# A lane inverse's last three copies and the next compaction are handed out later, at a raised pace

## The chip, the cores and the metric

One core of one Trainium2 chip runs the whole program as a single launch. The metric is the device time of that launch in microseconds (us), the median of three executions. The core has a matrix engine (TensorE, PE in the profile), three engines for elementwise work (VectorE or DVE, ScalarE or ACT, GpSimd or POOL), a queue that issues DMAs (SyncE, SP) and 16 DMA engines. Each engine works through its own queue in the order in which the program put instructions there.

## The reference, cut to what matters

Three parts follow one another. The first is a delta rule over 4 batches, 8 heads and 768 steps with 48-wide states:

```
for t in range(S):
    y[:, :, t] = einsum('bhd,bhde->bhe', q[:, :, t], state)
    v_old      = einsum('bhde,bhd->bhe', state, kt)
    state      = state + beta_t * einsum('bhd,bhe->bhde', kt, vt - v_old)
```

Its output, turned to 3072 tokens by 384, goes through an RMS norm and a gated feed-forward (`silu(xn @ w_gate) * (xn @ w_val) @ w_out`, inner width 1536), and then through a second feed-forward (`h = x @ w_in`, `h * tanh(softplus(h)) @ w_out`, inner width 2048). All of it is float32.

## The kernel before, in words

The 768 steps are cut into 12 rows of 64 steps (r = 0 to 11); two rows are a segment (sg = 0 to 5). Within a row the recurrence is solved with matrices. It needs, for each segment, the inverse of 32x32 triangular blocks for all heads. From segment 2 on that inverse is made by the lane generator `inlane(sg)`, nearly all of it on DVE: a compaction of the matrix A (`diagonal`, ACT at L621 and DVE at L622, into the tile comp), a transpose into N_, a scaling, small steps of 2 to 7 (below called s2 to s7), products and reduces of 8x8 blocks (p8 and r8, L653 and L689), products and reduces of 16x16 blocks (p16 and r16, L653 and L707), a scaling mulX (L709), a transpose into X11 (L714), a transpose into yc (L718), and last three ACT copies of yc into A (L720 to L722). Each step ends with a `yield` of a cost; one segment's yields add up to 31.45. Straight after the copies of one segment comes the compaction of the next. `merges(sg)` then makes, on PE with ACT copies between, the off-diagonal blocks (`merge32`: L734, an ACT copy Z at L738, L744, an ACT copy into A at L748); its four parts are handed out between the first steps of the next segment's inverse.

`chain_row(r)` is a row's own work, as a list of named stages. Those that matter here: r (residual, L935 on PE and L940 on DVE), q0 and q1 (transposes of the queries at L615, copied by ACT at L616), p (scores, L595 and DVE L605), nA and nB (norms of the keys of row r+4; nB ends with a DVE reciprocal at L555 and a POOL product at L556), c0 and c1 (transposes of those keys, L615), y (L953), X and Y (the former row's output to the feed-forward, L1054; ACT L1058 and L1060, POOL L1061 writes xl), v (L978, ACT L983), k (state update, L1027 on PE and L1032, tile sx, on DVE), o0 and o1 (L994), g (L595 and ACT L603).

`part_a` is the feed-forward of earlier rows for the first 512 inner columns: matmuls at L255 to L257 into two-step tiles pg and pv (DVE L313 and L316 and POOL L317 make hh and hl from them), and a down product at L289 to L291 in three units that share one PSUM tile pd; ACT copies pd into par (L1110) before the next unit may write pd.

For each row from 2 to 9 `merge` interleaves these streams: it always takes the stream whose handed-out cost is the smallest share of that stream's total. The row's chain has its own cost as total, `part_a` 11 units, and the lane `P["LANE"]`, 15.7 = 31.45 / 2. `until` stops the lane for a row once its running total has reached `upto`, which is 14.2 for row 2 and 15.7 more for each row after, and without limit in row 9. The order that results is the order of every engine's queue; nothing is reordered later. PSUM tiles of the chain come from five banks (tag pp): a matmul into a reused bank waits for whoever read it last.

After row 11 (at about 460 us) the kernel runs the rest of the gated feed-forward and the second feed-forward, with matmuls throughout.

Of the kernel before, what the change touches and what calls it, by code (L numbers as in the profile page):

```python
# [17 lines left out]


P = dict(  # L20
    XB=2, WE=16, RB=4, TB=3, LANE=15.7, CVT=9.0, CVB0=0, CVB1=1.238, CVC=4.4, PSD=1, NU=6, CVA=1, CVE=14.671, CVD=3.5, SQ=5,
    ROW="r nA q0 q1 S p T nB y X v Y k c0 o0 c1 o1 g".split(),
    R0="r q0 q1 p v k o0 o1 s0 s1 x0 x1 c0 c1 g".split(),
    R1="r nA q0 q1 y p nB v k o0 o1 s0 s1 x0 c0 c1 g".split(),
# [37 lines left out]
def merge(*streams):  # L62
    live = [[g, float(total), 0.0] for g, total in streams if total > 0]
    while live:
        s = min(live, key=lambda x: x[2] / x[1])
        try:
            s[2] += next(s[0])
        except StopIteration:
            live.remove(s)


def budget(gen, amount):
    done = 0.0
    while done < amount:
        try:
            w = next(gen)
        except StopIteration:
            return
        done += w
        yield w  # L80


def until(gen, total, target):
    while total[0] < target:
        try:
            w = next(gen)
        except StopIteration:
            return
        total[0] += w
        yield w  # L90


def delay(amount):
    for _ in range(int(amount)):
        yield 1.0
# [3 lines left out]
def kernel(  # L99
# [18 lines left out]
    NR = S // C  # L118
# [7 lines left out]
    QE = 3  # L126
    XB = P["XB"]

    def pool(name, bufs=1, **kw):
        kw.setdefault("reuse_waits", "tile")  # L130
        return tc.tile_pool(name=name, bufs=bufs, **kw)
# [11 lines left out]
    def seq(*gens):  # L143
        for g in gens:
            yield from g


    def prepare(get_pool, key, cut, act=True, low=None, **kw):
        return [prepare_half(half, get_pool, key, cut, act, low or nc.gpsimd, kw) for half in range(2)]
# [50 lines left out]
    def convs(pairs, at_once=0):  # L200
        depth = P["RB"]
        gens = [g for p in pairs for g in p]
        for g in gens[:depth]:
            next(g)
        yield 0.1
        for g in gens[:at_once]:
            next(g)
            yield 0.2
        for g in gens[:at_once]:
            next(g)  # L210
            next(g)
            yield 1.4
        for i, g in enumerate(gens[:at_once]):
            for g in gens[i + depth:i + depth + 1]:
                next(g)
            for _ in gens[i]:
                pass
            yield 0.1
        gens = gens[at_once:]
        next(gens[0])  # L220
        yield 0.2
        last = iter(())
        for i, g in enumerate(gens):
            if i + 1 < len(gens):
                next(gens[i + 1])
            for _ in range(2):
                next(g)
                yield 0.7
            if i + depth < len(gens):
                next(gens[i + depth])  # L230
            for _ in last:
                pass
            last = g
            yield 0.1
        for _ in last:
            pass

    def cols(w, m):
        return w.rearrange("(k p) f -> p k f", p=128)[:, :, m * 256:(m + 1) * 256], KD, 256

    def rows(w, m):
        return w.rearrange("(k p) f -> p k f", p=128)[:, 2 * m:2 * m + 2, :], 2, DM
# [4 lines left out]
    def need(*keys):  # L247
        assert done.issuperset(keys), set(keys) - done
# [80 lines left out]
    def x_tiles():  # L329
        return [xp.tile([128, KD, T], F32R, tag=tag, name=tag, bufs=XB) for tag in ("xh", "xl")]  # L330

# [6 lines left out]
    def phase_b1():  # L338
# [33 lines left out]
        even, odd, top = (qc[:, 192 + i:193 + i] for i in range(3))  # L372
        bnat = xp.tile([128, KD, T], F32R, tag="xl", name="bnat", bufs=XB).bitcast(F32)
        bnat = bnat.rearrange("p a b -> p (a b)")[0:32, 0:S]
# [40 lines left out]
        def flat(t):  # L415
            return t.bitcast(F32).rearrange("p a b -> p (a b)")
# [209 lines left out]
        def inlane(sg):  # L626
# [89 lines left out]
            yc = il.tile([128, 1024], F32, tag="pr", name="yc", bufs=2)  # L716
            Yc = yc.rearrange("p (u c) -> p u c", c=32)
            nc.vector.transpose(out=Yc.rearrange("p u c -> p c u"), in_=Nv)  # L718
            yield 2.0
            nc.scalar.copy(A[32:64, :, 32:64], Yc[32:64])  # L720
            nc.scalar.activation(out=A[:, :, 0:32], in_=Yc, func=ACTF.Copy, scale=h0[:, 0:1])
            nc.scalar.copy(A[96:128, :, 32:64], Yc[96:128])  # L722
# [169 lines left out]
        def lanes(ending):  # L892

            nc.gpsimd.memset(X_, 0.0)
            nc.gpsimd.memset(X_.rearrange("p (i x) -> p i x", x=33)[:, :, 0:1], 1.0)
            for sg in range(2, NSEG):
                done_of, due = 0.0, 2.5
                for w in inlane(sg):
                    yield w
                    done_of += w  # L900
                    if done_of >= due:
                        next(ending, None)
                        due += 2.0
                for _ in ending:
                    pass
                ending = merges(sg)
            left.append(ending)

        def chain_row(r):
# [135 lines left out]
            def to_x(bp):  # L1045
                need(("sx", r, bp))
                po, dg = xn[bp]
                if bp == 0:
                    need(*([("up", r - XB)] if r >= XB else []))
                    x_t[r].extend(x_tiles())  # L1050
# [52 lines left out]
        def cost(r):  # L1103
            return sum(cost_of(x) for x in order(r))
# [42 lines left out]
        spare = rp.tile([128, 16, 64], F32, tag="PT", name="spare")[:, :, 0:D]  # L1147
        sq = [xp.tile([128, KD, T], F32R, tag="xh", name="sq", bufs=XB) for _ in range(2)]
        sq = [flat(t)[:, 0:16 * D].rearrange("p (u d) -> p u d", d=D) for t in sq]
# [26 lines left out]
        for sg in range(1, NSEG):  # L1176
            for rl in range(2):
                r = 2 * sg + rl
                streams = [(chain_row(r), cost(r))]
                due = P["DUE"][r] if r < len(P["DUE"]) else P["DUE"][-1]  # L1180
                if due > 0:
                    off = 1.5 if r == 2 else 0
                    streams.append((seq(delay(off), budget(part_a, due)), off + due))
                if r < len(P["CVS"]):
                    streams.append((budget(cv, P["CVS"][r]), P["CVS"][r]))
                if r < len(P["CVS"]):
                    streams.append((budget(cv, P["CVS"][r]), P["CVS"][r]))
                if sg + 1 < NSEG:
                    upto = (r - 1) * P["LANE"] - 1.5 if r < NR - 3 else 999.0
                    streams.append((until(lane, laned, upto), P["LANE"]))  # L1190
                elif rl == 0:
                    st_i.close()
                    streams.append((seq(left.pop(), delay(7.0)), 13.0))
                    wbp.append(st_b.enter_context(pool("wbA")))
                    todo = [(c, m, cols(w, m)) for m in range(FA, NP1) for c, w in (("g", w_gate), ("v", w_val))]
                    todo += [("o", m, rows(w_out1, m)) for m in range(FA, NP1)]
                    gens = []
                    for i, (c, m, cut) in enumerate(todo):
                        if 2 * i < WE:
                            gens.append(prepare(lambda: wbp[0], (c, m), cut, tag="wb", bufs=WE))  # L1200
                        else:
                            gens.append(prepare(lambda: wbp[1], (c, m), cut, low=nc.vector, tag="wb", bufs=2 * len(todo) - WE))
                    cv = convs(gens)
                    streams.append((budget(cv, 0.75 * WE), 0.75 * WE))
                else:
                    streams.append((budget(cv, 0.75 * WE), 0.75 * WE))
                merge(*streams)
# [136 lines left out]
    WE = P["WE"]  # L1344
    with tc.manual_schedule():
        st_b, st_w, st_2 = ExitStack(), ExitStack(), ExitStack()
        rest = [phase_b1()]
        w2i = st_2.enter_context(pool("w2i", side="right"))
        tpc = st_2.enter_context(pool("tpc", side="right"))
        ps_u = st_2.enter_context(pool("ps_u", P["NU"], space=PSUM))  # L1350
        ps_d = st_2.enter_context(pool("ps_d", 8 - P["NU"], space=PSUM))
        last = phase_c()
        phase_b2(rest[0], lambda: next(last))
        st_w.close()
        for _ in last:
            pass
        st_2.close()
        st_b.close()
# [30 lines left out]
```

## Time and profile before

| | us |
|---|---|
| median of three executions | 1211.27 (1210.17 to 1212.03) |
| the profiled execution | 1213.2, its span 1211.1 |
| PE busy in the span | 1125.3 (93%) |
| DVE busy | 713.1 (59%) |
| ACT busy | 566.7 (47%) |
| POOL busy | 400.4 (33%) |

The span is the time from the first to the last instruction of the profiled execution. Shares over the whole span mix a first part (to about 460 us), in which all engines take part, with a second in which PE is busy nearly always. The granted clock is the clock that TensorE was given, 1.00 for 2.4 GHz and 0.50 for 1.2 GHz.

### The profile page before, as it was taken

What the parts mean: (1) busy time and instruction counts of PE and PEld (TensorE: products, weight loads), DVE (VectorE), ACT (ScalarE), POOL (GpSimd) and SP (SyncE); (2) the same over time, 40 slices, a digit from 0 to 9 for tenths busy, and PEclk for the clock granted to TensorE, in tenths of its full rate; (3) what the DMA queues carried; (4) which work ended last, traced back from release to release, by engine and by line L of the source; (5) the groups of instructions that cost most, each with busy time, mean ns of one, the idle gap of its engine ahead of it and who ended that gap; (6) DMA issues with size and microseconds to landing.
All of it is one profiled execution on the core that took longest, in us unless ns stands there. A gap on an engine that the chain in (4) does not pass through costs nothing.

```text
span 1211.1 us, 33707 instructions
## 1 busy us (share of the span) xinstructions
PE 1125.3 (93%) x14784; PEld 1095.4 (90%) x14784; DVE 713.1 (59%) x1148; ACT 566.7 (47%) x1075; POOL 400.4 (33%) x360
## 2 busy tenths in 40 slices
PE   5687698999998879999999999999999999999998
PEld 5677687889897878999999999989999999999998
DVE  6657898798868767555555553379334433333433
ACT  4355636566555654211121111054757655555672
POOL 2031134354522443234443433223323322232232
PEclk7666788999999979999999999999999999999999
DMA  9022333232224544333333322331011101111101
GB/s 161 3 67 54 96 81 68 68 94 73 77 60 116 170 132 144 105 116 126 126 119 105 105 92 92 120 130 53 27 40 41 40 18 38 38 40 40 40 1 27
DMA packets 120483, 95.08 MB, mean 79 GB/s; under 512 B 79856, under 2 KB 102896, under 8 KB 120336
## 3 DMA queue, kind: packets, MB, share of 16 engines
q1 hardware_dynamic: 108240, 69.32, 21.2%
q10 hardware_dynamic: 12096, 23.60, 6.0%
q8 instruction: 116, 1.90, 0.7%
q14 instruction: 31, 0.25, 0.1%
HBM read 64.59 MB, written 28.31 MB: 77 GB/s over the span
## 4 chain that ended last, share of the span: by engine, by line
PE 70%; DVE 17%; ACT 5%; issue 4%; POOL 2%; DMA 1%; SPq 1%; DVEq 0%; POOLq 0%; ACTq 0%
PE pd L1285 5%; PE pd L1286 5%; PE pd L1284 5%; PE ph L256 5%; PE ph L257 5%; PE ph L255 5%; PE pd L289 4%; PE pg L255 4%; PE pd L291 4%; PE pd L290 3%; PE pg L257 3%; PE pg L256 3%; PE pv L255 3%; PE pv L256 3%; PE pv L257 3%
## 5 line engine op out<-in xcount | busy, mean ns | idle before, releaser
L1332 POOL TENSOR_TENSOR gl<-t,gh 128x512 fp32r<-128x512 f32 x96 | 124.6, 1298 | 272.0 <-DVE gh L1331 269.9
L317 POOL TENSOR_TENSOR hl<-sg,hh 128x512 fp32r<-128x512 f32 x72 | 98.7, 1370 | 241.8 <-DVE hh L316 233.5
L255 PE MATMUL ph<-xh,wih 128*128 128x256 f32 x576 | 162.0, 281 | 2.9 <-DVE t L1328 2.9
L257 PE MATMUL ph<-xh,wil 128*128 128x256 f32 x576 | 162.0, 281 | 0.0
L256 PE MATMUL ph<-xl,wih 128*128 128x256 f32 x576 | 161.9, 281 | 0.0
L289 PE MATMUL pd<-hh,woh 128*128 128x256 f32 x420 | 122.3, 291 | 15.0 <-ACT par L1110 15.0
L1285 PE MATMUL pd<-wql,gh 128*128 128x384 f32 x384 | 129.6, 337 | 0.3
L1284 PE MATMUL pd<-wqh,gh 128*128 128x384 f32 x384 | 129.4, 337 | 0.5 <-DVE wqh L195 0.5
L1286 PE MATMUL pd<-wqh,gl 128*128 128x384 f32 x384 | 129.3, 337 | 0.0
L255 PE MATMUL pg<-xh,wgh 128*128 128x256 f32 x432 | 128.6, 298 | 0.3 <-ACT wgh L193 0.3
L307 ACT ACTIVATE sg<-pg 128x512 f32<-128x512 f32 x72 | 43.1, 598 | 183.1 <-PE pg L257 161.2
L255 PE MATMUL pv<-xh,wvh 128*128 128x256 f32 x432 | 126.4, 293 | 0.0
L257 PE MATMUL pg<-xh,wgl 128*128 128x256 f32 x432 | 124.8, 289 | 0.9 <-DVE wgl L196 0.9
L256 PE MATMUL pg<-xl,wgh 128*128 128x256 f32 x432 | 124.7, 289 | 0.8 <-POOL xl L1061 0.8
L257 PE MATMUL pv<-xh,wvl 128*128 128x256 f32 x432 | 122.4, 283 | 1.1 <-DVE wvl L196 1.1
L256 PE MATMUL pv<-xl,wvh 128*128 128x256 f32 x432 | 122.5, 284 | 0.0
L290 PE MATMUL pd<-hl,woh 128*128 128x256 f32 x420 | 119.7, 285 | 0.0
L291 PE MATMUL pd<-hh,wol 128*128 128x256 f32 x420 | 119.6, 285 | 0.0
L1328 DVE TENSOR_TENSOR t<-t,ph 128x512 f32<-128x512 f32 x96 | 65.2, 679 | 82.1 <-ACT t L1326 82.1
L255 PEld LDWEIGHTS ph<-xh,wih 128*128 128x128 f32 x576 | 109.2, 190 | 3.1 <-DVE t L1328 3.1
L313 DVE TENSOR_TENSOR sg<-sg,pv 128x512 f32<-128x512 f32 x72 | 49.4, 686 | 102.5 <-PE pv L257 96.4
L256 PEld LDWEIGHTS ph<-xl,wih 128*128 128x128 f32 x576 | 109.1, 189 | 0.0
(213 smaller groups left out, 2913.0 us busy)
## 6 DMA issues: line engine op xcount, KB each, us to landing
raw<-in_moe_w_out_dram SPq DMA_DIRECT2D x28, 384.0 KB, 3.5
raw<-in_moe_w_in_dram SPq DMA_DIRECT2D x16, 384.0 KB, 4.1
kh<-in_k_dram SPq DMA_DIRECT2D x24, 192.0 KB, 3.9
qp<-in_q_dram SPq DMA_DIRECT2D x24, 192.0 KB, 3.6
v<-in_v_dram SPq DMA_DIRECT2D x48, 96.0 KB, 3.1
raw<-in_moe_w_gate_dram SPq DMA_DIRECT2D x12, 384.0 KB, 3.3
raw<-in_moe_w_val_dram SPq DMA_DIRECT2D x12, 384.0 KB, 3.7
xh_d<-xh SPq DMA_DIRECT2D x12, 384.0 KB, 2.4
```

The lines of the kernel that those rows point to most:

```text
L255: nc.tensor.matmul(ps[:, f, :], wh[:, kt, sl], xh[:, kt, :], start=(kt == 0), stop=False)
L256: nc.tensor.matmul(ps[:, f, :], wh[:, kt, sl], xl[:, kt, :], start=False, stop=False)
L257: nc.tensor.matmul(ps[:, f, :], wl[:, kt, sl], xh[:, kt, :], start=False, stop=(kt == KD - 1))
L289: nc.tensor.matmul(ps, wh[:, f, sl], hh[:, f, :], start=(i + f == 0), stop=False)
L290: nc.tensor.matmul(ps, wh[:, f, sl], hl[:, f, :], start=False, stop=False)
L291: nc.tensor.matmul(ps, wl[:, f, sl], hh[:, f, :], start=False, stop=last)
L317: nc.gpsimd.tensor_tensor(out=hl, in0=sg, in1=hh.bitcast(F32), op=ALU.subtract)
L1284: nc.tensor.matmul(ps, gh[:, f, sl], wh[:, f, :], start=(m + f == 0), stop=False)
L1285: nc.tensor.matmul(ps, gh[:, f, sl], wl[:, f, :], start=False, stop=False)
L1286: nc.tensor.matmul(ps, gl[:, f, sl], wh[:, f, :], start=False, stop=last)
L1328: nc.vector.tensor_tensor(out=t, in0=t, in1=ps, op=ALU.mult)
L1332: nc.gpsimd.tensor_tensor(out=gl, in0=t, in1=gh.bitcast(F32), op=ALU.subtract)
```

## The change

The yield after the transpose into yc grows from 2.0 to 8.2, the pace LANE from 15.7 to 18.8 (half of the new sum 37.65), and the constant by which `upto` falls short of the pace from 1.5 to 3.0. So `upto` is 15.8 for row 2 and 18.8 more for each row after. No instruction is added or removed.

```diff
-    XB=2, WE=16, RB=4, TB=3, LANE=15.7, CVT=9.0, CVB0=0, CVB1=1.238, ...
+    XB=2, WE=16, RB=4, TB=3, LANE=18.8, AFTER=6.2, LD=3.0, CVT=9.0, CVB0=0, CVB1=1.238, ...
...
             nc.vector.transpose(out=Yc.rearrange("p u c -> p c u"), in_=Nv)
-            yield 2.0
+            yield 2.0 + P["AFTER"]
             nc.scalar.copy(A[32:64, :, 32:64], Yc[32:64])
...
                 if sg + 1 < NSEG:
-                    upto = (r - 1) * P["LANE"] - 1.5 if r < NR - 3 else 999.0
+                    upto = (r - 1) * P["LANE"] - P["LD"] if r < NR - 3 else 999.0
                     streams.append((until(lane, laned, upto), P["LANE"]))
```

## Rows read from the trace of the kernel before

**Rows 1.** Waits of PE, 160 to 450 us: waited for, us in total, times, longest.

```profile
PE pd L289 <- ACT par L1110: 13.2, 4, 4.3
```

**Rows 2.** PE in order of time: start, us, instruction, count, [idle before <- releaser].

```profile
200.46 1.04 PE L615 MATMUL pp<-ident,qp 128*128 128x128 f32 x8
205.53 0.58 PE L289 MATMUL pd<-hh,woh 128*128 128x256 f32 x1 [4.04 <-ACT par L1110]
...
269.17 0.39 PE L289 MATMUL pd<-hh,woh 128*128 128x256 f32 x1 [2.45 <-ACT par L1110]
...
328.49 0.39 PE L289 MATMUL pd<-hh,woh 128*128 128x256 f32 x1 [2.42 <-ACT par L1110]
...
383.18 1.20 PE L734 MATMUL pp<-X,A 32*32 32x32 f32 x64 [1.06 <-DVE X L714]
...
388.90 0.24 PE L744 MATMUL pp<-A,Z 32*32 32x32 f32 x2 [2.91 <-ACT Z L738]
```

**Rows 3.** ACT in order of time, at the start of row 4.

```profile
200.79 1.04 ACT L720 COPY A<-yc 32x1024 f32<-32x1024 f32 x1 [4.05 <-DVE yc L718]
...
204.07 1.15 ACT L621 ACTIVATE comp<-A,h 128x1024 f32<-128x1024 f32 x1
```

**Rows 4.** DVE in order of time: the first yc, and sx of rows 4, 6, 8.

```profile
198.69 2.07 DVE L718 STREAM_TRANSPOSE yc<-N__166 128x1024 f32<-128x1024 f32 x1
...
228.13 1.02 DVE L1032 TENSOR_TENSOR sx<-sx,pp 128x384 f32<-128x384 f32 x2 [7.74 <-PE pp L1027]
...
287.44 1.02 DVE L1032 TENSOR_TENSOR sx<-sx,pp 128x384 f32<-128x384 f32 x2 [4.11 <-PE pp L1027]
...
348.86 1.02 DVE L1032 TENSOR_TENSOR sx<-sx,pp 128x384 f32<-128x384 f32 x2 [8.91 <-PE pp L1027]
```

**Rows 5.** Stretches: length, busy PE, PEld, DVE, ACT, POOL, granted clock, DMA, GB/s.

```profile
165.00:200.00 35.00, 34.04 (x745) 31.45 (x744) 34.62 (x40) 18.96 (x51) 16.68 (x15) 0.99 0.33 76
...
205.00:210.00 5.00, 4.47 (x72) 4.24 (x74) 4.71 (x4) 2.86 (x7) 0.51 (x1) 0.50 0.02 4
210.00:215.00 5.00, 5.00 (x122) 4.68 (x120) 3.09 (x11) 1.53 (x3) 3.69 (x3) 0.63 0.01 3
...
330.00:335.00 5.00, 5.00 (x141) 4.62 (x140) 4.06 (x5) 1.77 (x4) 0.00 (x0) 0.68 0.02 3
...
460.00:1211.00 751.00, 741.77 (x5674) 739.83 (x5673) 359.96 (x586) 311.03 (x482) 249.11 (x208) 1.00 0.23 73
```

**Rows 6.** DVE in order of time, behind sx of row 4: p8, r8, p8.

```profile
229.07 1.06 DVE L653 TENSOR_TENSOR pr<-N__166,X__167 128x512 f32<-128x512 f32 x1
...
231.10 0.68 DVE L689 TENSOR_REDUCE T<-pr 128x64 f32<-128x512 f32 x1
231.70 1.93 DVE L653 TENSOR_TENSOR pr<-X__167,T 128x512 f32<-128x512 f32 x1
```

**Rows 7.** DVE in order of time: the reciprocal of row 3's nB.

```profile
183.92 0.24 DVE L555 RECIPROCAL rn<-nr 128x16 f32<-128x16 f32 x1
```

**Rows 8.** Stretches of row 3, columns as in rows 5.

```profile
184.05:187.20 3.15, 3.15 (x81) 2.97 (x80) 3.12 (x4) 3.08 (x10) 2.81 (x1) 1.00 0.48 90
193.90:196.76 2.86, 2.86 (x89) 2.56 (x83) 2.78 (x4) 2.67 (x7) 2.51 (x2) 1.00 0.45 52
```

**Rows 9.** POOL in order of time, row 3.

```profile
184.39 2.94 POOL L556 TENSOR_TENSOR kh<-kh,rn 128x768 f32<-128x768 f32 x1 [1.66 <-PE pp L978]
...
187.29 3.23 POOL L1061 TENSOR_TENSOR xl<-xf,xh 128x384 fp32r<-128x384 f32 x2
```

**Rows 10.** PE in order of time, row 3: c0, a pg, c1.

```profile
188.06 0.60 PE L615 MATMUL pp<-ident,kh 128*128 128x128 f32 x4
...
190.58 0.38 PE L256 MATMUL pg<-xl,wgh 128*128 128x256 f32 x1 [0.79 <-POOL xl L1061]
...
191.96 0.66 PE L615 MATMUL pp<-ident,kh 128*128 128x128 f32 x4 [0.17 <-DVE sx L1032]
```

**Rows 11.** PE in order of time: row 4's k.

```profile
226.95 1.14 PE L1027 MATMUL pp<-ve,kh 64*64 64x48 f32 x62 [0.64 <-ACT xf L1060]
```

More of the change, by code (lines that the diff above doesn't have):

```diff
@@ L20 @@
 P = dict(
-    XB=2, WE=16, RB=4, TB=3, LANE=15.7, CVT=9.0, CVB0=0, CVB1=1.238, CVC=4.4, PSD=1, NU=6, CVA=1, CVE=14.671, CVD=3.5, SQ=5,
+    XB=2, WE=16, RB=4, TB=3, LANE=18.8, AFTER=6.2, LD=3.0, CVT=9.0, CVB0=0, CVB1=1.238, CVC=4.4, PSD=1, NU=6, CVA=1, CVE=14.671, CVD=3.5, SQ=5,
     ROW="r nA q0 q1 S p T nB y X v Y k c0 o0 c1 o1 g".split(),
```

## The prediction

> **What bounds the kernel now.** I read the table of stretches first. From 460 us on PE is busy 741.77 of 751 us at the full granted clock, 2.4 GHz [rows 5]: what the first 460 us lose or save arrives at the end unchanged, as long as nothing of that part waits for a transfer, and the change moves no DMA to another place in its row. The waits of PE come next. Between 160 and 450 us the largest is 13.2 us in four pieces: a down product (L289) waits for the copy par that frees pd [rows 1]. PE in order of time shows three of them at the starts of rows 4, 6 and 8: 4.04, 2.45 and 2.42 us [rows 2] (the fourth lies in rows 10 and 11, without a lane). ACT in order of time says why: the three yc copies stand at the head of the row's queue, ACT idles 4.05 us before the first of them until DVE has made yc, and only after the copies and the compaction does par's turn come [rows 3]. The first wait costs twice: behind it the granted clock is 0.50, its 1.2 GHz level, from 205 to 210 us and 0.63 from 210 to 215 [rows 5], worth 4.47 x 0.50 = 2.2 and 5.00 x 0.37 = 1.9 us of PE's work, 4.1 together. Behind the 2.42 us wait it is 0.68 for 5 us, 1.6 lost; behind the 2.45 us wait the matmul took 0.39 us against 0.58 at the first [rows 2], no loss. At row 10's start PE waits for X11 (1.06) and for Z, which stands behind the copies on ACT (2.91) [rows 2].
>
> DVE in order of time is the reader's last view. In rows 2 and 3 DVE never rests (34.62 of 35 us [rows 5]). In rows 4, 6 and 8 it idles 7.74, 4.11 and 8.91 us before sx, because PE has not yet done k [rows 4].
>
> **The change, part by part.** Stepping the rule "smallest share next" through the yields gives both orders. The copies do not move against the row's chain: in both kernels the rows 4, 6 and 8 open with the first residual, one `part_a` unit, the copies and the compaction. What moves is everything of the lane before them. In the odd row:
>
> ```
> before: ... nB p16 ... k r16 .. p16 c0 r16 o0 mulX .. trX11 c1 .. o1 g .. trY | copies
> after:  ... p16 .. r16 T nB p16 ... p16 r16 mulX .. Y k trX11 .. c0 trY o0 .. c1 .. o1 g .. | copies
> ```
>
> The even row takes one r16 over from the odd one. Ahead of its k the lane now has p8, r8, p8 more: 1.06 + 0.68 + 1.93 = 3.7 us [rows 6] (in row 8: r8, p8, r8, 0.68 + 1.06 + 0.68 = 2.4). And the first part of the merges, L734 (about 1.2 us by [rows 2]), stands before the down product that waits for par instead of behind it.
>
> *Row 3 and the start of row 4.* DVE has no idle time there, so packing the lane forward only pushes the row's own DVE work back; yc still ends at 198.69 + 2.07 = 200.8 [rows 4], par still comes at about 205.5. The row's instructions fall behind: ahead of nB's reciprocal (183.92 [rows 7]) now stand one p16 and one r16 more, 3.1 us [rows 8]. POOL's key scaling ended at 184.39 + 2.94 = 187.3 [rows 9], 0.7 before c0 used it at 188.06 [rows 10]; now it ends at 190.4, so PE waits 2.3. xl behind it on POOL ends 3.1 later, at 193.6; PE, after c0 and o0 (1.6 us), reaches it at 192.0 and waits 1.6 instead of 0.79 [rows 10]; I take 1.4, because the second xl no longer runs beside the same DVE product. sx falls behind r16, p16, r16 and mulX (0.68 as [rows 6] and 2.78 [rows 8], 3.5); PE is 2.9 later by then, so c1's 0.17 [rows 10] becomes 0.7. Together 4.4 where 0.96 stood, +3.4. PE comes out of q1 at 201.5 + 3.4 = 204.9, does L734 to 206.1 and finds par done. Before, par let it go at 205.53 with L734 to come, 206.7. Net -0.6 (bounds: +2 if the second xl and sx each cost a us more; -2.3 if c0's wait is covered). The clock: three waits of 0.7 to 2.3 instead of one of 4.04. Full or half rate behind them lies between -4.1 and 0; nearest rows are the two waits of 2.4, one with a loss of 1.6 and one without. I take half, -2.0.
>
> *Rows 4 to 6.* PE's wait for k's bank (0.64 [rows 11], and one like it in row 6) goes, since the last bank then comes from a merge copy ahead of xf on ACT: -1.3 for both (bounds -1.3 and 0). DVE reaches sx 3.7 us of lane work later, paid from 7.74 idle: 4.04 left, less what PE gains (2.6 to 6). So sx stays PE's to release, or within a us of it. From sx to yc DVE then has 3.7 less to do, so yc, and what row 5 needs of DVE (3.1 to 3.5 later in order), come out 0.2 to 0.6 ahead of PE's pace in place of behind it: no new wait as in row 3. yc is there before ACT reaches the copies; the copies and compaction (about 4.5 us, 200.79 to 205.2 in [rows 3]) run while PE does the last units, the transposes and L734. The wait of 2.45 goes. If the cover fails it comes back whole, less 1.2.
>
> *Rows 6 to 8.* The same with 4.11 idle against 3.7, margin 0.4, or 1.4 if one counts that nB's reciprocal waited a us for POOL here and now comes later. 2.42 and the clock's 1.6 go: -4.0 (bounds 0 and -4.0).
>
> *Rows 8 to 10.* Here the copies stay behind all of row 9's other work, and L734 does not move. yc comes 2.4 earlier (8.91 idle in row 8 pays [rows 4]); X11's 1.06 goes, and of Z's 2.91 about 1.6 stays: -2.4 (bounds -4.0 and 0). The clock behind it I leave as it is.
>
> Sum: -0.6 - 2.0 - 1.3 - 2.45 - 4.0 - 2.4 = -12.8. The profiled execution, 1213.2 with a span of 1211.1, would take 1200.4; the median of the runs, 1211.27 and 1.9 below it, 1198.5.
>
> The Trainium skill bears on the thin margin. Rows first: the p8 at 231.70 took 1.93 us, the p8 of the same 512 elements at 229.07 1.06 [rows 6], so a product can cost 0.87 more than its like. The Trainium skill (SBUF — State Buffer, "Who interferes with whom") says that a DVE instruction with two SBUF inputs and a GpSimd instruction that reads SBUF exclude each other, and that the later one waits for the whole of the earlier. By that rule a lane packed into less of the row meets POOL's work more often, and the margin of row 6 could go; the result is the second rival's, and no row here shows how often.
>
> **Rivals.** (1) *Only L734 pays.* If DVE gets nothing back in rows 5 and 7 (sx released late by as much as was moved ahead of it), yc comes no earlier against PE, and what is left is 1.2 us of cover at three row starts and perhaps row 9's 2.4: -3.6 to -6, 1205 to 1207.7. For it: DVE is busy without a break in every odd row. Against it: the idle time before sx in rows 4 and 8 is twice what is moved.
>
> (2) *Slower: DVE becomes what rows 5 and 7 wait for.* It decides where DVE reaches sx in rows 4 and 6 more than about 1 us after PE has done k. Then c0, xl and c1 wait there as in row 3, 4.4 each, against 2.45 and 2.42 saved: +3.9. The split waits hold the clock at its lower level as the wait at row 4 did, 4.1 a row for three rows against 4.1 + 1.6 now: +6.6. With -0.6 and -2.4: +7.5, 1218.8. For it: the margin of 0.4 to 1.4 in row 6, and PE gains that shorten DVE's idle time. Against it: rows 4 and 8 have 7.74 and 8.91.
>
> (3) *It does not do what it says.* The copies are nominally 6 units later, but stand at the same place of the next row; if the new waits in the odd rows (4.4) just replace those at the starts (4.04, 2.45, 2.42) with the clock as it is, nothing moves: about 1211. The trace shows idle time that speaks against it in two of three rows.
>
> **How the numbers follow.** The forecast (-8 to -18) has 0.60, rival 1 0.18, rival 2 0.13, rival 3 0.09. This kernel's measurement tells about 0.2% (2.4 us) from no change. Faster takes the forecast, rival 1, and a little of rival 3: 0.80; same most of rival 3, 0.07; slower rival 2, 0.13. The low end takes every term at its better bound, -2.3 - 4.1 - 1.3 - 2.45 - 4.0 - 4.0 = -18: 1193. The high end takes in rival 1 and stops short of rivals 2 and 3: 1208.
>
> **What would show it right or wrong.** Right: L289's waits for par at the starts of rows 4, 6, 8 below 0.5 us; ACT's wait for yc gone at rows 6 and 8 and still about 4 at row 4; new waits of PE in row 3 at c0 (for kh), xl and sx, about 4 together; DVE's idle time before sx under 2 us in rows 4 and 6; L734 ahead of the second down product. Wrong: PE waits at c0, xl or sx in rows 5 and 7 too; a granted clock below 1 in the odd rows; waits for par that stay; gains before 400 us that rows 10 and 11 give back to their weight preparation.

## The result, and the profile after

The changed kernel takes 1197.95 us (median of four runs, 1196.49 to 1199.74) against 1210.72 for the kernel before on the same chip (four runs, 1207.94 to 1212.03). The ratio is 0.9887 with an interval of 0.9871 to 0.9903: 13.7 us faster. The forecast was 1198.5, faster.

The profiled execution took 1199.74 us, its span 1197.7. Busy times over the span hardly differ from before; what differs is idle time of PE and its clock in the first 450 us. Behind that the two kernels are alike, as the table of stretches after the change shows (columns as in [rows 5]; its last line answers to the last of [rows 5]). The first four lines come back below.

```profile
185.00:190.00 5.00, 4.43 (x74) 4.18 (x75) 4.97 (x7) 1.90 (x4) 2.53 (x2) 0.53 0.08 15
190.00:195.00 5.00, 5.00 (x96) 4.56 (x97) 4.90 (x8) 2.08 (x7) 3.06 (x2) 0.79 0.56 145
205.00:210.00 5.00, 5.00 (x169) 4.59 (x169) 4.32 (x3) 4.41 (x9) 1.27 (x1) 1.00 0.42 82
215.00:220.00 5.00, 4.34 (x24) 4.30 (x24) 4.83 (x7) 1.86 (x5) 1.48 (x1) 0.66 0.02 6
447.00:1198.00 751.00, 741.59 (x5668) 739.63 (x5667) 359.68 (x585) 310.61 (x481) 249.91 (x208) 1.00 0.23 73
```

So the gain is read from the start of each row's k (L1027), the row's fixed mark. From the two traces, in us:

| from k of row to k of row | before | after | change | predicted |
|---|---|---|---|---|
| 2 to 4 | 65.8 | 63.6 | -2.2 | -3.25 |
| 4 to 6 | 59.3 | 56.7 | -2.6 | -3.1 |
| 6 to 8 | 62.4 | 57.15 | -5.2 | -4.0 |
| 8 to 10 | 66.0 | 62.2 | -3.85 | -2.4 |
| 2 to 10 | 253.5 | 239.65 | -13.85 | -12.75 |

(The 1.3 for waits on xf, one in row 4 and one in row 6, is split between the first two lines of the forecast.) Row 2's k comes 0.7 later and the part after row 10's k is 0.25 shorter.

Three things limit how the table may be read. First, one merge part (L744, 1.2 us) stands behind row 8's k before and ahead of it after; for the same work the third line is -6.4 and the fourth -2.65. PE in order of time, before and then after:

```profile
348.74 1.20 PE L744 MATMUL pp<-A,Z 32*32 32x32 f32 x64
```

```profile
335.31 1.20 PE L744 MATMUL pp<-A,Z 32*32 32x32 f32 x64
```

Second, the change costs 1.7 us in row 2, ahead of its k, which the table leaves out. From row 2's scores (L595) to its k the kernel before takes 9.17 us (151.02 to 160.19), the changed one 10.84 (150.04 to 160.88). Lane steps now stand on DVE ahead of the row's weight preparation, ACT waits for the latter, and ve, which k needs, comes behind that on ACT. PE before, PE after, ACT before, ACT after:

```profile
151.02 1.98 PE L595 MATMUL pp<-QT,kT 64*64 64x64 f32 x64 [8.26 <-ACT QT L616]
...
160.19 0.31 PE L1027 MATMUL pp<-ve,kh 64*64 64x48 f32 x2 [1.32 <-ACT ve L983]
```

```profile
150.04 1.99 PE L595 MATMUL pp<-QT,kT 64*64 64x64 f32 x64 [8.26 <-ACT QT L616]
```

```profile
159.25 0.51 ACT L193 CAST woh<-t 128x384 fp32r<-128x384 f32 x1 [5.91 <-DVE t L182]
```

```profile
159.94 0.51 ACT L193 CAST woh<-t 128x384 fp32r<-128x384 f32 x1 [7.59 <-DVE t L182]
```

Third, one execution is not a measurement of rows 2 to 4. A later run (the DVE load in the changed kernel, below) has the order of the change up to row 4's k and takes 60.95 us there, where the profiled execution of the change took 63.63. From row 4's k on, the four traces with this order and nothing added agree within 0.3 us a line.

PE in order of time after the change, at the places of [rows 2] and at new waits:

```profile
160.88 0.31 PE L1027 MATMUL pp<-ve,kh 64*64 64x48 f32 x2 [3.07 <-ACT ve L983]
...
185.42 0.44 PE L978 MATMUL pp<-v,A 64*64 64x48 f32 x2 [2.44 <-DVE PT L605]
...
204.87 1.04 PE L615 MATMUL pp<-ident,qp 128*128 128x128 f32 x8
...
205.83 1.20 PE L734 MATMUL pp<-X,A 32*32 32x32 f32 x64
...
206.96 0.39 PE L289 MATMUL pd<-hh,woh 128*128 128x256 f32 x1
...
215.66 0.21 PE L734 MATMUL pp<-X,A 32*32 32x32 f32 x2 [0.95 <-issue]
...
266.40 0.39 PE L289 MATMUL pd<-hh,woh 128*128 128x256 f32 x1
...
370.31 0.39 PE L255 MATMUL pv<-xh,wvh 128*128 128x256 f32 x1 [2.02 <-DVE sg L313]
...
377.24 1.19 PE L744 MATMUL pp<-A,Z 32*32 32x32 f32 x62 [0.34 <-ACT Z L738]
...
400.53 1.15 PE L1027 MATMUL pp<-ve,kh 64*64 64x48 f32 x64
```

The line at 160.88 is row 2's k. At the starts of rows 4 and 6, L734 (205.83 in row 4) now stands ahead of the second down product, and that product (206.96, 266.40) waits for nothing, where [rows 2] had 4.04 and 2.45. Row 8 is the same. In their place stand one wait of 2.44 in row 3 and one of 2.02 in row 9. The waits for par that are left (4.28 and 3.42) lie in rows 10 and 11.

ACT in order of time after the change; the first line answers to [rows 3]:

```profile
201.17 1.04 ACT L720 COPY A<-yc 32x1024 f32<-32x1024 f32 x1
...
205.52 0.35 ACT L1110 COPY par<-pd 128x256 f32<-128x256 f32 x1
...
261.18 1.04 ACT L720 COPY A<-yc 32x1024 f32<-32x1024 f32 x1 [0.59 <-DVE yc L718]
```

ACT's wait for yc, 4.05 at row 4 before, is gone there, 0.59 at row 6 and 0.56 at row 8. Note that at row 4 par itself ends at 205.87, no earlier than PE had it before (205.53): PE no longer waits there because PE comes later (its query transposes start at 204.87 instead of 200.46).

DVE in order of time after the change (the sx lines answer to [rows 4]):

```profile
184.68 1.28 DVE L605 TENSOR_TENSOR PT<-pp,mpos 128x512 f32<-128x512 f32 x2
...
225.95 1.02 DVE L1032 TENSOR_TENSOR sx<-sx,pp 128x384 f32<-128x384 f32 x2 [4.01 <-PE pp L1027]
...
235.47 1.02 DVE L940 TENSOR_TENSOR v<-v,pp 128x384 f32<-128x384 f32 x2 [1.47 <-PE pp L935]
...
282.65 1.02 DVE L1032 TENSOR_TENSOR sx<-sx,pp 128x384 f32<-128x384 f32 x2 [1.06 <-PE pp L1027]
...
292.20 1.02 DVE L940 TENSOR_TENSOR v<-v,pp 128x384 f32<-128x384 f32 x2 [1.50 <-PE pp L935]
...
339.56 1.02 DVE L1032 TENSOR_TENSOR sx<-sx,pp 128x384 f32<-128x384 f32 x2 [3.96 <-PE pp L1027]
```

The idle time of 7.74, 4.11 and 8.91 before sx has shrunk to 4.01, 1.06 and 3.96. It was not all used up, and in the odd rows DVE has new idle time at their first residual (L940).

### The profile page after: what moved, and what is told of

It reads as the page before. It is cut to its first block, busy times and chain, and to the rows that moved or that the text cites. A ratio compares the mean times of both kernels' runs of the same rounds, so it can differ in the third digit from the quotient of the medians.

```text
span 1197.7 us, 33711 instructions
## 1 busy us (share of the span) xinstructions
PE 1116.6 (93%) x14784; PEld 1087.3 (91%) x14784; DVE 713.5 (60%) x1148; ACT 566.4 (47%) x1075; POOL 404.2 (34%) x360
## 4 chain that ended last, share of the span: by engine, by line
PE 76%; DVE 14%; ACT 3%; issue 3%; POOL 2%; DMA 1%; SPq 1%; DVEq 0%; POOLq 0%; ACTq 0%
PE pd L1285 5%; PE pd L1286 5%; PE pd L1284 5%; PE ph L257 5%; PE ph L255 5%; PE ph L256 5%; PE pv L255 4%; PE pg L255 4%; PE pd L289 4%; PE pg L256 4%; PE pg L257 4%; PE pv L257 4%; PE pv L256 4%; PE pd L290 4%; PE pd L291 4%
## 5 line engine op out<-in xcount | busy, mean ns | idle before, releaser
L317 POOL TENSOR_TENSOR hl<-sg,hh 128x512 fp32r<-128x512 f32 x72 | 105.2, 1460 | 238.3 <-DVE hh L316 231.5
L289 PE MATMUL pd<-hh,woh 128*128 128x256 f32 x420 | 120.4, 287 | 7.7 <-ACT par L1110 7.7
L257 PEld LDWEIGHTS ph<-xh,wil 128*128 128x128 f32 x576 | 109.1, 189 | 0.0
```

Of the source, the lines that this page charges most:

```text
L257: nc.tensor.matmul(ps[:, f, :], wl[:, kt, sl], xh[:, kt, :], start=False, stop=(kt == KD - 1))
L289: nc.tensor.matmul(ps, wh[:, f, sl], hh[:, f, :], start=(i + f == 0), stop=False)
L317: nc.gpsimd.tensor_tensor(out=hl, in0=sg, in1=hh.bitcast(F32), op=ALU.subtract)
```

## The experiments

The letters in the quoted expectations stand for these theories. **A**, the prediction's: the lane is packed into DVE's idle time, yc is early, L734 covers the rest, and the waits for par go with their clock. **B**: the cover by L734 is nearly all of it. **C**: the clock behind the waits costs nothing. **D**: half the delay does as much as the whole. **E**: handing the copies out later is in itself the gain. **F**: the new order costs time in rows 2 to 4, where DVE has no rest. All ratios are against the kernel before on the same chip, with their interval; differences from the change are differences of these ratios. "k to k" is the stretch from row 2's k to row 10's (253.5 before, 239.65 after) in the one profiled execution of each run.

### The cover alone, and the change without it

The kernel before, with L734 ahead of the second down unit and the rest of the order unchanged:

```diff
-            yield 2.0      # after the transposes trN
+            yield 1.4
...
-            yield 1.1      # after the product mulN
+            yield 1.7
```

> The kernel before with one order changed: at the starts of rows 4, 6 and 8 the first merge part (L734) stands ahead of the down product that waits for par, as in the kernel after; the lane's pace is the old one. Theory A (the gain comes from lane work packed into DVE's idle time before sx, so that yc is early): only about 1.2 us of cover at each start. L289's waits for par fall from 4.04, 2.45, 2.42 to about 2.9, 1.3, 1.2 us, ACT still waits 2.4 to 4 us for yc; time 2 to 6 us below the kernel before, so 7 to 11 us above the kernel after. Theory B (L734's place is what pays): 9 us or more below the kernel before.

Measured 0.9934 (0.9919 to 0.9949), 8.0 faster, between the two. Its PE in order of time, at rows 4, 6 and 8, and its first stretch:

```profile
204.48 0.39 PE L289 MATMUL pd<-hh,woh 128*128 128x256 f32 x1 [2.91 <-ACT par L1110]
...
264.90 0.39 PE L289 MATMUL pd<-hh,woh 128*128 128x256 f32 x1 [1.27 <-ACT par L1110]
...
323.71 0.39 PE L289 MATMUL pd<-hh,woh 128*128 128x256 f32 x1 [1.35 <-ACT par L1110]
```

```profile
200.00:215.00 15.00, 11.87 (x346) 10.83 (x344) 11.10 (x20) 9.83 (x16) 6.83 (x4) 0.89 0.22 55
```

Each wait is 1.1 to 1.2 shorter, as the 1.2 us of L734 say, while ACT still waits 4.06, 2.41 and 2.48 for yc. But the granted clock of the stretch from 200 to 215 us rose from 0.66 to 0.89 with a wait that is still 2.91. k to k is 247.1, 6.4 of the 8.0; the rest lies outside these rows. So the cover is worth its own length and, in this execution, most of the clock behind the first wait, more than A had for it.

The other way round, the changed kernel with L734 back behind the down product:

```diff
-            yield 2.0      # after the transposes trN
+            yield 2.6
...
-            yield 1.1      # after the product mulN
+            yield 0.5
```

> The kernel after with L734 put back behind the down product at the starts of rows 4, 6 and 8; pace and copies as in the kernel after. Theory A: yc stays early; in the kernel after PE is through with the query transposes 0.6 us before par is written at row 6, so each start shows a wait for par of 0.5 to 1 us and the time rises by 1 to 3 us against the kernel after. Theory B: the waits come back at 2 us or more each and the time rises by 8 us or more.

Measured 0.9928 (0.9913 to 0.9943), 8.7 faster than before and some 5 slower than the change; again between. k to k is 241.8, only 2.1 above the change; in the two profiled executions most of the rest is a later row 2 (k at 162.82), ahead of all that this edit moves. PE in order of time, rows 6 and 8, then a stretch of row 8:

```profile
265.68 0.39 PE L289 MATMUL pd<-hh,woh 128*128 128x256 f32 x1 [0.57 <-ACT par L1110]
...
323.31 0.39 PE L289 MATMUL pd<-hh,woh 128*128 128x256 f32 x1 [0.59 <-ACT par L1110]
...
327.90 0.24 PE L744 MATMUL pp<-A,Z 32*32 32x32 f32 x2 [0.68 <-ACT Z L738]
```

```profile
330.00:335.00 5.00, 5.00 (x141) 4.68 (x141) 4.69 (x11) 1.82 (x4) 0.00 (x0) 0.73 0.20 75
```

Waits of 0.57 and 0.59, not 2.4, with the packing alone. In row 8 such a wait, with 0.68 at Z, was followed by a stretch at 0.73 of the clock. Packing alone gives 8.7, cover alone 8.0, both 13.7: 3 us less than their sum, since both act on the same waits.

### What the clock behind the waits costs

The kernel before, with products of the identity into a spare bank while PE would wait for par (18 of them in each of rows 4, 6, 8):

```diff
+                    if r in (4, 6, 8):
+                        fill = bank(KD, 128)
+                        for _ in range(18): nc.tensor.matmul(fill[:, 0, :], ident, ident)
```

> The kernel before with 18 added matmuls of the identity (about 2.3 us at the full clock), into a PSUM bank that nobody reads, behind the query transposes of rows 4, 6 and 8, where PE waits for par. It measures the clock's share by itself. Theory A (half the loss at row 4 is the lower clock): L289's waits fall to about 1.7, 0.1 and 0.1 us, the copies and yc stay where they are, and the granted clock behind them stays at 1.00; the time falls by 3 to 6 us (4.1 and 1.6 were counted as lost to the clock). Theory C (the clock behind the waits costs nothing because DVE's chain sets the pace anyway): within 1 us of the kernel before.

Measured 0.998 (0.997 to 0.999), 2.4 faster, below A's 3 to 6. The fill was too long for two of its three places: PE in order of time shows 4.18 us for 18 products, not the 2.3 that was expected; each makes two records.

```profile
200.74 4.18 PE L925 MATMUL pp<-ident 128*128 128x128 f32 x36
```

In rows 6 and 8 that outlasts waits of 2.4 by some 1.7 us each, so about 3.5 are lost there. The next one fits the fill to the wait, 17 in row 4 and 9 in rows 6 and 8:

```diff
-                        for _ in range(18): ...
+                        for _ in range(17 if r == 4 else 9): ...
```

> The kernel before with added identity matmuls at the starts of rows 4, 6 and 8 as in the first such run, but 17 in row 4 and 9 in rows 6 and 8. There 18 took 4.2 us and not 2.3, so they outlasted the waits of rows 6 and 8 by 1.6 us each; -5.7 for the clock and +3.2 for that make the -2.4 measured. With the right lengths (3.9 and 2.1 us) theory A expects the clock's 5.7 us alone: 4 to 7 us below the kernel before. Theory C (the clock is worth nothing): 0 to 1 us.

Measured 0.9961 (0.9946 to 0.9976), 4.7 faster, k to k 248.9 (-4.6). PE in order of time and the two stretches:

```profile
200.37 3.96 PE L925 MATMUL pp<-ident 128*128 128x128 f32 x34
```

```profile
200.00:215.00 15.00, 14.70 (x393) 13.76 (x392) 11.09 (x20) 9.95 (x16) 6.84 (x4) 1.00 0.21 55
...
325.00:340.00 15.00, 14.83 (x446) 13.82 (x444) 9.50 (x19) 9.72 (x24) 1.00 (x1) 1.00 0.19 49
```

The same two stretches of the kernel before:

```profile
200.00:215.00 15.00, 10.96 (x200) 10.18 (x200) 10.42 (x19) 8.54 (x13) 5.47 (x4) 0.66 0.14 28
...
325.00:340.00 15.00, 12.57 (x335) 11.60 (x335) 10.89 (x21) 8.41 (x16) 1.27 (x1) 0.89 0.21 55
```

PE is held up as long as before, only busy; ACT's waits for yc stay (4.06, 2.46, 2.45), and no useful work is added. The 4.7 are what the clock gives on balance: C falls, and in sum the prediction's 4.1 + 1.6 for the clock behind the waits was near. By rows it was not even: row 2's k to row 4's is 4.1 shorter and row 6's to row 8's 3.7, while the two other stretches are 1.1 and 2.1 longer, which these runs do not explain.

The 3.7 is more than the 1.6 that the prediction priced at row 8, because the clock of the kernel before fell a second time in that row, about two waits of 0.37 and 0.39 us at v (341.3 and 342.9):

```profile
340.00:345.00 5.00, 4.24 (x120) 3.89 (x114) 0.00 (x0) 4.32 (x11) 1.00 (x1) 0.84 0.08 16
345.00:350.00 5.00, 5.00 (x145) 4.77 (x145) 1.14 (x3) 2.27 (x8) 0.99 (x1) 0.82 0.59 151
```

That is another 4.24 x 0.16 + 5.00 x 0.18 = 1.6 us, some of it behind row 8's k (347.66).

### The size of the delay, and the copies alone

Half the delay:

```diff
-LANE=18.8, AFTER=6.2, LD=3.0
+LANE=17.275, AFTER=3.1, LD=2.25
```

> The kernel after with half the delay (3.1 in place of 6.2), the pace 17.275 and the lead 2.25. Ahead of the even rows' k there is then one p8 (1.06 us) more than before in place of p8, r8, p8 (3.7), and L734 stays behind the down product. Theory A: yc comes about 1 us earlier at rows 6 and 8, so the waits for par there are about 1.4 us and at row 4 about 3.5; 2 to 6 us below the kernel before. Theory D (any delay of the copies is enough): as fast as the kernel after, within 2 us.

Measured 0.9934 (0.9919 to 0.9949), 8.0 faster, outside A's 2 to 6; k to k 243.0. PE's waits for par at rows 4, 6 and 8 are 0.56, 0.58 and 0.55, where A had expected 1.4 and up; ACT waits only 0.55 to 0.58 for yc at these rows. So half the delay already makes yc almost early enough, yet the time is 5.7 us behind the change, which contradicts D too. Of the stretches, the last one, row 8's k to row 10's, differs most from the change (64.98 against 62.17); PE waits 1.77 for Z there. In row 3 its PE waits 0.53 for PT, 0.35 for kh, 1.30 for xl and 0.35 for sx: the last three are the victims that the prediction named for the whole delay.

One and a half times the delay:

```diff
-LANE=18.8, AFTER=6.2, LD=3.0
+LANE=20.375, AFTER=9.3, LD=3.75
```

> The kernel after with one and a half times the delay (9.3), the pace 20.375 and the lead 3.75. Ahead of the even rows' k DVE then has about 4.3 us more than in the kernel before (3.7 in the kernel after), and in row 3 PT stands behind one more reduce and product (about 2.7 us). Theory A: no wait for par is left to remove at rows 6 and 8; v's wait in row 3 grows to about 5 us and DVE's idle time before sx in row 6 (1.06 us) is used up; 1 to 6 us above the kernel after. Theory D (more delay, more gain): below the kernel after.

Measured 0.9931 (0.9914 to 0.9947), 8.4 faster and 5.3 behind the change, at the upper end of what A expected. DVE's idle time before sx is down to 0.52 and 0.54 us in rows 4 and 6, PE waits 0.90 and 0.91 for xl in rows 5 and 7, and row 9's wait for sg has grown from 2.02 to 3.33. v's wait in row 3 did not grow to 5 as expected; it is 2.13.

The copies moved behind par in the kernel before. The lane's pace rises with the added cost, so that, as the expectation says, a little less of it lies ahead of the even rows' k:

```diff
-    LANE=15.7
+    LANE=16.575
...
             nc.vector.transpose(out=Yc.rearrange("p u c -> p c u"), in_=Nv)
             yield 2.0
+            yield 1.7
             nc.scalar.copy(A[32:64, :, 32:64], Yc[32:64])
...
-                    upto = (r - 1) * P["LANE"] - 1.5 if r < NR - 3 else 999.0
+                    upto = (r - 1) * P["LANE"] - 2.35 if r < NR - 3 else 999.0
```

> The kernel before with the copies themselves handed out later: a cost of 1.7 is yielded between the transpose into yc and the three copies (pace 16.575, lead 2.35), which puts the copies and the compaction behind the first down unit and its par copy at the starts of rows 4, 6 and 8. No lane work moves ahead of the even rows' k; there is less of it there than before. Theory A (what counts is that yc is early): PE no longer waits for par, but the query copies now stand behind the copies of yc on ACT, so the scores (L595) wait about as long as the down product did; within 4 us of the kernel before. Theory E (it is enough that the copies are not ahead of par): 8 us or more below the kernel before.

Measured 1.0047 (1.0031 to 1.0063), 5.7 slower, somewhat more than the 4 that A allowed. The wait for par went, and PE in order of time shows where it went to: the row's own scores wait for QT, which ACT (L616) now makes behind the copies (row 4; rows 6 and 8 have 3.83 and 3.10).

```profile
208.27 1.99 PE L595 MATMUL pp<-QT,kT 64*64 64x64 f32 x64 [3.82 <-ACT QT L616]
```

E falls: with a yc that comes no earlier, later copies exchange one victim for another here, at a loss. A place behind the query copies too was not tried.

### Rows 2 to 4

The changed kernel with the old order up to row 3, the new one from there:

```diff
-            yield 2.0 + P["AFTER"]
+            yield 2.0 + (P["AFTER"] if sg > 2 else 0.0)
...
-                    upto = (r - 1) * P["LANE"] - P["LD"] if r < NR - 3 else 999.0
-                    streams.append((until(lane, laned, upto), P["LANE"]))
+                    pace = P["LANE"] if r > 3 else 15.7
+                    upto = (r - 1) * pace - 1.5 if r <= 3 else 31.45 + (r - 3) * pace - P["LD"] - 0.05 if r < NR - 3 else 999.0
+                    streams.append((until(lane, laned, upto), pace))
```

> The kernel after with rows 2 and 3 (segment 2) in the order of the kernel before, pace and delay of the kernel after from row 4 on. In the kernel after row 3 pays: v waits 2.6 us for the scores' PSUM banks, which DVE frees late at PT, and the clock is low for about 7 us behind it; k of row 3 comes 5.8 us later than before. Theory A (DVE has no idle time in rows 2 and 3, so yc of segment 2 comes no earlier and the wait only changes place): row 3 as before, then a wait for par of about 2.9 us at row 4's start and a low clock behind it; within -2 to +4 us of the kernel after. Theory F (row 3's loss is avoidable by the old order): 4 to 6 us below the kernel after.

Measured 0.9858 (0.9841 to 0.9874), 17.2 faster than before, the fastest of all; by the ratios 3.5 faster than the change, between A and F, with intervals that just overlap. k to k is 237.6. PE in order of time:

```profile
158.17 0.31 PE L1027 MATMUL pp<-ve,kh 64*64 64x48 f32 x2 [1.89 <-ACT ve L983]
...
203.49 0.57 PE L289 MATMUL pd<-hh,woh 128*128 128x256 f32 x1 [2.91 <-ACT par L1110]
```

The wait for par at row 4 is back (2.91, less the cover), and still the way from row 2's k to row 4's, 61.60, is 2.0 us shorter than in the profiled execution of the change. But the run with the DVE load in the changed kernel has the change's order there and takes 60.95, so the 2.0 do not show that the old order is better between these marks. What the traces do show is row 2 ahead of its k: 9.17 us from its scores in this run, as in the kernel before, against 10.84 and 10.85 in two executions of the new order. From row 2's scores to row 4's k it is 70.77 here, 74.47 and 71.80 there. So F holds for at least 1 us by the traces; its 4 to 6 are not shown. Row 2's scores start at 149.00 here and at 151.02 in the kernel before, with the same order up to there; over the twelve traces that leave the low parts on DVE this start lies between 148.76 and 151.97, so that part can't be counted for the order.

The changed kernel with its row 3 relieved in another way: the low parts of the first pieces of w_out are made on POOL instead of DVE (`low=nc.vector` dropped from that `prepare`).

```diff
-            gens.append(prepare(lambda: wa, ("o", m), rows(w_out1, m), low=nc.vector))
+            gens.append(prepare(lambda: wa, ("o", m), rows(w_out1, m)))
```

> The kernel after with the subtractions that make the low parts of the first four output-weight pieces (wol at L196, rows 2 and 3, about 3 us of DVE) on POOL in place of DVE. Theory A (row 3's loss comes from DVE being full in rows 2 and 3): everything DVE does from there to yc comes 2 to 3 us earlier, v's wait for PT falls from 2.6 to below 1 us, and the time falls by 2 to 6 us against the kernel after. If DVE is not what row 3 waits for: within 1 us of the kernel after.

Measured 0.9869 (0.9855 to 0.9884), 15.9 faster, about 2 below the change with intervals that overlap; k to k 237.2. v's wait for PT in row 3 is 0.83 against 2.44, and the clock from 185 to 195 us is 1.00 instead of 0.53 and 0.79:

```profile
186.61 0.31 PE L978 MATMUL pp<-v,A 64*64 64x48 f32 x2 [0.83 <-DVE PT L605]
```

Part of that fall would have come without the edit: the run with the DVE load, whose row 3 has the order of the change, waited 1.15 at v and also kept the clock at 1.00. PE and the stretch of that run:

```profile
185.85 0.31 PE L980 MATMUL pp<-v,A 64*64 64x48 f32 x2 [1.15 <-DVE PT L607]
```

```profile
180.00:225.00 45.00, 41.95 (x1060) 38.60 (x1060) 41.63 (x61) 29.61 (x69) 21.38 (x16) 1.00 0.33 82
```

What the edit does is seen from row 2's k: v starts 23.3 us behind it, against 24.5 and 24.65 in the two executions without the edit. So that start is set by how much of DVE's work lies ahead of PT. The edit also has a price in row 2. ACT in order of time waits 6.86 for a low part on POOL where it waited 2.80 for the one on DVE, and the copies of the queries stand behind it; the scores wait 12.30 for them instead of 8.26.

```profile
153.14 0.55 ACT L167 ACTIVATE t<-raw 128x384 f32<-128x384 f32 x1 [6.86 <-POOL wol L196]
```

Both remedies together (half the delay in rows 2 and 3, low parts on POOL):

```diff
-            yield 2.0 + P["AFTER"]
+            yield 2.0 + (P["AFTER"] if sg > 2 else 3.1)
...
+                    pace = P["LANE"] if r > 3 else 17.275
+                    upto = (r - 1) * pace - 2.25 if r <= 3 else 34.55 + (r - 3) * pace - P["LD"] - 0.05 if r < NR - 3 else 999.0
...
-            gens.append(prepare(lambda: wa, ("o", m), rows(w_out1, m), low=nc.vector))
+            gens.append(prepare(lambda: wa, ("o", m), rows(w_out1, m)))
```

> The kernel after with two changes to rows 2 and 3: half the delay for segment 2 alone (the order of the half dose there, the order of the kernel after from row 4 on), and the low parts of the first output weights on POOL. Theory A: from k of row 2 to k of row 4 the kernel after takes 63.1 us; the old order, the half dose and the low parts on POOL each take 61.0 to 61.1 by themselves, since a PE without waits takes about that long, so together they give little more: 2 to 4 us below the kernel after, level with the old order in segment 2. If the two add up: 5 us or more below the kernel after.

Measured 0.9893 (0.9872 to 0.9913), level with the change, where 2 to 4 below it was expected. k to k is the shortest of all, 235.5, but row 2's k starts at 163.56, 2.7 later than in the change: most of what rows 2 to 10 won was lost ahead of them, by the same wait for POOL (6.79). The simple version with the old order in rows 2 and 3 has the lowest time of all runs.

### How much margin DVE has

Rival 2 hung on a margin of 0.4 to 1.4 us before sx of row 6. The changed kernel with 8 transposes of a spare tile on DVE ahead of sx in rows 4, 6 and 8:

```diff
+                if r in (4, 6, 8):
+                    for _ in range(8): nc.vector.transpose(out=pad, in_=pad)
```

> The kernel after with eight transposes of a spare 128x256 tile in place, about 4 us of DVE, put ahead of sx in rows 4, 6 and 8. It takes away DVE's idle time there, which in the kernel after is 4.0, 1.1 and 4.0 us. Theory A (the packed lane is paid from that idle time): nothing at rows 4 and 8, sx of row 6 comes 3 us late, yc of row 8 with it, and the wait for par at row 8 comes back with 2 to 3 us; 2 to 5 us above the kernel after. If DVE's idle time before sx does not matter: within 1 us.

Measured 0.9882 (0.9855 to 0.9909): no different from the change, and the expectation fell. DVE and then PE in order of time, row 6:

```profile
278.93 3.79 DVE L1034 STREAM_TRANSPOSE pad<-pad 128x256 f32<-128x256 f32 x8
282.65 0.98 DVE L1037 TENSOR_TENSOR sx<-sx,pp 128x384 f32<-128x384 f32 x2
```

```profile
278.63 1.40 PE L1029 MATMUL pp<-ve,kh 64*64 64x48 f32 x64
```

DVE reaches sx 2.6 us after PE's k ends (280.03), and 1.3 after it in row 4, both past the 1 us from which rival 2 was to decide. From row 6's k to row 8's only 0.5 us is lost (57.7 against 57.15), and PE's waits at c1 in rows 5 and 7 stay at 0.34 each, as in the change. The load was paid from the second idle time: DVE's 1.47 and 1.50 at the odd rows' L940 became 0.29 and 0. In row 6 that is 1.06 + 1.50 = 2.6 us of the 3.8. The remaining 1.2 cost 0.5.

The same load in the kernel before:

> The kernel before with the same eight transposes ahead of sx in rows 4, 6 and 8, where DVE idles 7.7, 4.1 and 8.9 us. Theory A: they fit into the idle time, sx, yc and the waits for par stay where they are; within 1.5 us of the kernel before. If DVE's amount of work is the bound by itself: 10 us or more above it (three times about 4).

Measured 1.0004 (0.9989 to 1.0018): no change, as expected. DVE still idles before sx, 4.04 in row 4, 1.75 in row 6 and 2.79 in row 8:

```profile
287.90 1.02 DVE L1037 TENSOR_TENSOR sx<-sx,pp 128x384 f32<-128x384 f32 x2 [1.75 <-PE pp L1029]
```

So the idle time in [rows 4] was free to take: 3.8 us of work put there per even row costs nothing, and work that no later wait hangs on gains nothing either.

## Why the prediction was right

**Rows 4 to 8, the core: right.** DVE's idle time before sx shrank by 3.7, 3.05 and 4.95 us, yc of rows 6 and 8 came early, and L289's waits for par went from 2.45 and 2.42 to nothing. The two waits on xf went, as said. Row 4's 4.04 went too, as forecast without an earlier par: the rows' other waits brought PE there later. The fill shows that the clock is a term of its own (-4.7).

**Rows 6 to 8: a term too small.** For the same work the gain is 6.4, outside the bounds of 0 to 4.0. The forecast had 2.42 for the wait and 1.6 for the clock. It left out the clock's second fall in row 8 and v's waits of 0.37 and 0.39 (above), about 2 us together. In the kernel before with the DVE load the clock did not fall that second time (1.00 from 340 to 350 us), so this part varies between executions. Rows 4 to 6 gave 2.6 of 3.1, with a wait of 0.34 at c1 in row 5 (0.35 in row 7) that was not foreseen.

**Rows 2 to 4: right in sign, the wait misnamed, row 2 left out.** The prediction had PE wait at c0, xl and sx, 4.4 together. Measured is 2.6 at v (L978), for PT on DVE, whose products empty the banks that v writes; at c0, xl and c1 no wait is seen. The step that failed is the order of victims: it followed kh through POOL, and kh did come as much later as forecast (the reciprocal at 187.00, 3.1 behind [rows 7]), but on DVE PT stands ahead of that reciprocal, was pushed back too (184.68, 3.5 later than before), and PE needs it first. PE lost its time there and came later to all the rest. The clock term of -2.0 was a half between two cases, and the two executions show about these: in the profiled one 205 to 215 us is full, but 185 to 195 us loses 4.43 x 0.47 + 5.00 x 0.21 = 3.1 (first two stretches after the change) and 215 to 220 us 4.34 x 0.34 = 1.5, so 4.6 where it was 4.1; in the one with the DVE load nothing is lost from 180 to 225 us. Hence -2.2 in the table, against -3.25; the two loaded runs, whose load lies behind the mark, differ by 4.05 (65.00 and 60.95). The second failed step is that the prediction had only the odd row's and the next row's order change and put row 2 itself at nothing: it costs 1.7 ahead of its k.

**The cover by L734: mis-sized.** The prediction priced it at 1.2 us a row, 3.6 for three. Alone it gave 8.0, and taken from the change it costs 5. The forecast's sum did not suffer, because cover and packing overlap by some 3 us and it counted each wait once.

**Rows 8 to 10: right.** Z's wait fell from 2.91 to 0.34 (1.6 was forecast to stay) and X11's 1.06 went, though sg now holds pv up for 2.02 in row 9, which was not foreseen. For the same work the gain is 2.65 against 2.4.

**The sum.** The core mechanism is right, but that the total is off by only a microsecond is partly luck: too much was forecast for rows 2 to 6 and too little for row 8. Of the signs that were to show it right, three did not come: ACT's wait of about 4 at row 4 (none; yc ended at 199.63 and ACT came to it later), the waits at c0, xl and sx in row 3, and DVE's idle time under 2 us in row 4 (4.01). One sign of being wrong did come in row 3: a granted clock below 1 in an odd row.

**Rival 1** falls: with the packing alone the waits for par are 0.57 and 0.59, and the time is 8.7 below the kernel before.

**Rival 2: rightly not chosen, for a reason partly wrong.** Its price was never tried, but its point of decision is shown wrong: with sx 1.3 and 2.6 us behind k next to nothing happened. The prediction counted one place at which DVE rests in a pair of rows, and there are two: DVE also waits for PE at the odd row's residual (L940). The risk of the slower side showed with a longer delay instead (one and a half times: 5.3 lost against the change). Rival 3 falls, since the waits at the row starts went and no equal ones took their place from row 4 on.

**Open.** Why half the delay, with short waits in all three rows, is 5.7 us behind: k to k says 3.35 of it, 2.8 of them between row 8's k and row 10's; the rest is not settled. Nor is what makes rows 2 to 4 of the same order take 63.63 us in one execution and 60.95 in another; PE reached v later in the second (its clock from 160 to 180 us was 0.83 against 0.91) and waited less there, but why is not shown.

## What to carry to other kernels

Where an in-order engine makes the matmul engine wait, look for the late operand at the head of its queue and make that one earlier out of another engine's idle time; here, putting the work behind the victim only found the next victim. Price a wait with the clock behind it (4.7 us here against 8.9 us of waits), and apply a reordering where the engine that pays has idle time; check every stage that the new order touches, also the first. When a margin is thin, count all its places of rest up to the next deadline, not only the first. Before a stretch of a few microseconds is explained from two traces, look whether two executions of one order agree there, and whether the same work lies between the marks.

## What the runs showed of the hardware

The length of one wait alone does not tell whether the clock falls. A gap of 0.95 us stands at the head of a stretch at 0.66 of the clock (215 to 220 us after the change); a gap of 1.10 at the same place of the run with the DVE load was followed by 1.00. The kernel before came out of a wait of 2.45 us [rows 2] with the clock at 1.00 from 265 to 275 us, and out of one of 2.42 with 0.68.

A product of the identity with itself in f32, 128x128, makes two records and took 0.23 us (3.96 / 17), while eight transposes against the same identity took 1.04 us, 0.13 each.

The DVE product of [rows 6] that took 1.93 us, 0.87 more than its like, started at 231.70 while a POOL product was running, to 232.61. The 0.91 us from its start to POOL's end and the 1.06 of its like make 1.97, so it looks held until POOL was done. POOL in order of time, before:

```profile
231.33 1.28 POOL L317 TENSOR_TENSOR hl<-sg,hh 128x512 fp32r<-128x512 f32 x1 [3.36 <-DVE hh L316]
```
